# Two layers of linear attention and squared-ReLU MLP: a sixth row buffer, two row statistics traced into the last feature pair, and a norm's last transposes ordered behind the dense block's last rows

## The chip, the cores and the metric

The kernel runs on one core of one Trainium2 chip. The metric is the device time of one execution in microseconds (us). A profile of one execution gives, beside its time, every instruction of each engine: TensorE (PE), its weight loads (PEld), VectorE (DVE), ScalarE (ACT), GpSimd (POOL) and SyncE (SP), which issues most DMAs.

## The reference

The input has 2048 rows of 576 values. Two layers, with the same weights, follow one another; each is an attention part and a dense part, each behind a layer norm without gain, and added to its input.

```python
def _A_ref(x, wqkv, w_phi, wo):                 # H = 32 heads of Dh = 18
    q, k, v = ... x @ wqkv ...
    pq = einsum("bhsd,hdf->bhsf", q, w_phi); pk = einsum("bhsd,hdf->bhsf", k, w_phi)
    phi_q = concatenate([softmax(pq), softmax(-pq)]); phi_k = concatenate([softmax(pk), softmax(-pk)])
    kv = einsum("bhsf,bhsd->bhfd", phi_k, v); z = einsum("bhsf->bhf", phi_k)
    num = einsum("bhqf,bhfd->bhqd", phi_q, kv); den = einsum("bhqf,bhf->bhq", phi_q, z)[..., None] + 1e-6
    return (num / den) ... @ wo

def _B_ref(x, w1, b1, w2, b2):                  # F = 4608
    r = max(x @ w1 + b1, 0)
    return (r * r) @ w2 + b2

x = x + _A_ref(_layernorm(x), ...); x = x + _B_ref(_layernorm(x), ...)      # layer one
x = x + _A_ref(_layernorm(x), ...); x = x + _B_ref(_layernorm(x), ...)      # layer two
```

The attention has no causal mask: the sums kv and z of a layer need the keys and values of all 2048 rows before the first output row can be made.

## The kernel before, in words

**Tiling.** The 2048 rows are four blocks of 512, each of four row tiles of 128. A row tile is a buffer x of 128 partitions by 576 float32. For a matmul, every operand is split into a high part (rounded to the matmul's type) and a low part (the rest), and each product is made of three: high by high, high by low, low by high. The 4608 hidden values of the dense part are 36 features of 128.

**Order within a layer.** In layer one the blocks go in the order 3, 2, 0, 1 and in layer two in the order 1, 0, 3, 2. First comes the attention output of the order's first block (`barrier`). Then the dense part of that block (`g_mlp`) is traced, and into it the attention of the second block is woven (`back_first`), norm included. Then comes the dense part of the second block, with the attention of the third and fourth block woven in (`back_second`). Last come the dense parts of the third and fourth block together (`g_pair`). Its 18 steps (`products`, one for each pair of features) make the hidden values of both blocks with fewer products than two separate blocks would need, finish the third block's rows and put the fourth block's hidden values aside in memory; `seconds` then reads them back and makes the fourth block's down-projection, feature by feature, with loads of weights (m_pr, `load_wide`) and of hidden values (m_pg, `load_high`) three features ahead. In layer one, `back_keys` is woven into `seconds`: for the blocks 3, 2 and 0, which are finished by then, it makes layer two's norm, values v and keys k. In layer two nothing is woven there.

**What sets the order on an engine.** The order in which the program is traced gives priorities; a planner then lays out each engine's instructions by the time at which it reckons them ready. On top of that, `tc.issue_after(ins)` puts what is traced in its block behind `ins` on the engine of `ins`, without a wait between engines. `weave(main, other, rate)` traces one step of `main` after the other, each of which pays `rate`, and draws steps of `other`, each of which costs what it yields; what is left of `other` is traced at the end (`drain`). `chained` wraps a woven generator so that its instructions on DVE, ACT and POOL stay in the order in which they are traced, step behind step; its `strict` form, which `back_keys` has, also puts them behind the PE instruction that was traced last.

**Buffers.** Tiles of one tag take turns in a fixed number of buffers; a tile whose turn it is waits until the last user of the buffer's old tile is done. The row tiles have the tag "x", with five buffers: the rows of a norm, the rows to which the dense part's result is added (named x or m_px), and a few temporary tiles. In PSUM the tag "w" has two banks.

**The norm.** `g_norm` (L452) handles four row tiles. For each, `begin` fetches the row and takes two half statistics (L438) and their aggregate (L441) on DVE, and two small POOL steps. `scale` writes the normed row: four chunks of 128 columns (L469, named n_3n for block 3 of layer two) and the rest (L470, n_3e). `transpose` turns the four chunks on PE (L480, into n_3p) and `split_main` splits them into high (ACT, L488) and low (DVE, L489, n_3l); `transpose_rest` (L494) turns the rests of two row tiles. With `fine`, as in `back_keys`, these are separate steps: two statistics ahead of the first scaling, and always one ahead; each statistics step costs 2.0, each scaling 1.6, and behind them follow six crossings (0.3) and splits (0.9). Without `fine`, as for the norm at the end of an attention (`g_out`, L999), one step holds the scaling of one row tile and the transposes of the one before; the last of the five steps holds the fourth row tile's four transposes and the second two rests.

**The places that the change touches.** In `g_mlp` (L1189 to L1215) the last feature's rows are made by row tile: L1159 holds the matmuls of the row tiles (m_3acc for block 3), L1154 and L1150 those of the columns beyond 512 (`features`). Then come four transposes (L1209) and the additions to the rows (L1212 and L1214). L1132 makes the next dense block's hidden values (m_2ph). In `g_pair`, L1471 and L1481 are `features` and `by_rows`; in `last_rows`, m_px is loaded, gets its additions (L1516 and L1520) and is written to xs (L1522). The rows x0 to x3 of layer two's first norm (L1767) are those of block 3, written to xs long before; they share the buffers of tag "x" with the four m_px. In the main loop (L1848 to L1854) a first step of `back_keys` is drawn in the last of the 18 steps, behind the last low split of the hidden values (`paired`, L1463), and a second one behind the additions of L1516 (`added`):

```python
        for k, _ in enumerate(products):
            if k == NP - 1:
                with tc.issue_after(dense["paired"].ins):
                    next(back, None)
        with tc.issue_after(dense["added"].ins):
            next(back, None)
        weave(seconds, back, 0.85)
```

The weights of v (w_3v0h to w_3v1l, four pieces, L406) are drawn within `back_keys`, beside the norm's steps, by `g_load`, which puts each piece behind the DMA that was traced last on SP.

Of the kernel before, what the change touches and what calls it, by code (L numbers as in the profile page):

```python
# [21 lines left out]
def layers_kernel(  # L22
# [75 lines left out]
        for _ in gen:  # L98
            pass

    def weave(main, other, rate):

        due = 0.0
        for _ in main:
            due += rate
            while due >= 1.0:
                cost = next(other, other)
                if cost is other:
                    break
                due -= cost or 1.0  # L110
        drain(other)

    def pipeline(n, stages, costs):

# [674 lines left out]

    def phi_products(layer, e, name, tag="qk"):  # L790
        zb = sums[layer]["zb"]
        ms = [sb.tile([P, D], F32, tag=tag, name=f"{name}{s}", bufs=5) for s in range(2)]
        for s in range(2):
            (nc.gpsimd if s else nc.vector).tensor_mul(ms[s], e[:, s], zb[:, s])
        return ms
# [30 lines left out]
    def phi_late(layer, er, ph, name):  # L826

        zb, ms, us = sums[layer]["zb"], {}, {}
        for t in range(NT // 2, NT):
            ms[t] = [sb.tile([P, D], F32, tag="x", name=f"{name}m{t}{s}", bufs=5) for s in range(2)]  # L830
            us[t] = sb.tile([P, 2, H], F32, tag="u", name=f"{name}u{t}")
            ph.append(er[t][0])

        def product(t, s):
            return (nc.gpsimd if s else nc.vector).tensor_mul(ms[t][s], er[t][0][:, s], zb[:, s])

        def total(t, s):
            nc.vector.tensor_reduce(us[t][:, s], ms[t][s].rearrange("p (h d) -> p h d", d=DH), op=ALU.add, axis=AX.X)

        def factors(t):  # L840
            phi_factors(us[t], er[t][1])

        def scale(t, s):
            phi_scale(*er[t], (s,))

        return product, total, factors, scale
# [18 lines left out]
    def g_out(layer, b, ph, dst, name, parts=1, pause=None, behind=None, norm=None, mid=None, costs=(None, None)):  # L865
# [59 lines left out]
                return two + [wpiece(wo, HP, f"{name}o1", heads=True, low=nc.gpsimd)]  # L925

        def rows_in(t):
            x = sb.tile([P, D], F32, tag="x", name=f"{name}x{t}", bufs=5)
            nc.sync.dma_start(x, x_in[b * TB + t * P : b * TB + (t + 1) * P] if layer == 0 else xs[b][t])
            return x  # L930

# [64 lines left out]
            nc.sync.dma_start(xm[b][t], x)  # L996

        if not xs_of:
            yield from paced((norm or g_norm)(x_after, dst, f"{name}n", keep), costs[1])  # L999
            return  # L1000

        spare["tags"] = [f"acc{i}" for i in range(NC)]
# [87 lines left out]
    def g_mlp(layer, b, x, after, name, rest=None, then=None):  # L1090
# [108 lines left out]
        if then:  # L1199
            then()  # L1200
        for t in range(NT):
            x = sb.tile([P, D], F32, tag="x", name=f"{name}x{t}", bufs=5)
            nc.sync.dma_start(x, xm[b][t])
            after.append(x)
        by_rows(NF - 1, range(2), range(3))
# [1 line left out]
        p3 = pt.rearrange("p (t d) -> p t d", d=P)  # L1207
        for t in range(NT):
            nc.tensor.transpose(p3[:, t], yt[:, t * P : (t + 1) * P], ident)  # L1209
        by_rows(NF - 1, range(2, NT), range(3))  # L1210
        for t, x in enumerate(after):
            nc.vector.tensor_add(x[:, :R], acc[t][:, :R], x[:, :R])  # L1212
        for t, x in enumerate(after):
# [71 lines left out]
    def g_norm_second(x_of, dst, name, then):  # L1285

        ops, full, made = {}, [], {}

        def two(t):
            return t[:, : HK * TB].rearrange("p (c n) -> p c n", c=HK)  # L1290

        def prepare():
            rests = cst.tile([P, 2 * D], F32, name=f"{name}f", tag="zb")
            for a, k in enumerate(("b11", "b21")):
                cols = slice(a * HK * TB, (a + 1) * HK * TB)
                hi, lo = (sb.tile([P, 2 * D], F32, tag="E", name=f"{name}{k}{p}", bufs=4)[:, : HK * TB] for p in "hl")
                nc.sync.dma_start(hi, pth[:, cols])
                nc.sync.dma_start(lo, ptl[:, cols])
                full.append(rests[:TP, a * TB : (a + 1) * TB])
                nc.sync.dma_start(full[a], ptt[:, a * TB : (a + 1) * TB])  # L1300
                ops[k] = [two(hi.bitcast(F32R)), two(lo.bitcast(F32R))]

        def rest():
            for k in ("t1", "t3", "t4"):
                tags = ("wraw", "wraw") if k == "t4" else TAGS_A
                pair = [sb.tile([P, NC * HP], F32R, tag=tag, name=f"{name}{k}{p}", bufs=2)
                        for tag, p in zip(tags, "hl")]
                ops[k] = [two(p) for p in pair]
            x = xt_tiles(name)
            ops["b22"] = [x[p][:, :HK] for p in "hl"]  # L1310
            ops["t2"] = [x[p][:, HK:KC] for p in "hl"]
            for k in ("b11", "b21", "t1", "t2"):
                ops[k].append(sb.tile([GW, TB], F32R, tag="ft", name=f"{name}{k}t", bufs=4)[:TP])
            ops["t3"].append(sb.tile([P, TB], F32R, tag="olt", name=f"{name}t3t", bufs=1)[:TP])
            ops["t4"].append(sb.tile([P, KC * P], F32, tag="xn", name=f"{name}t4t").bitcast(F32R)[:TP])
            ops["b22"].append(x["h"][:TP, KC])
            for k, f in zip(("b11", "b21"), full):
                split_tail(ops[k][2], f)

        def split_tail(op, src):  # L1320
            nc.scalar.activation(op, src, AF.Copy)
            nc.vector.tensor_sub(op[TW : 2 * TW], src[TW : 2 * TW], op[TW : 2 * TW].bitcast(F32))

        def combine(new, c11, c21):
            b12, b22 = new
            temps = [sb.tile([P, D], F32, tag="x", name=f"{name}u{i}", bufs=5) for i in range(2)]
# [36 lines left out]

        prepare()
        yield from g_norm_halves(x_of, name, then, (main, split_main), (tail, split_tails), (0.3, 3.6, 2.4))
        dst.update(ops)

    def g_pair(layer, blocks, x, after, name):
# [120 lines left out]
        def last_rows(b):  # L1489
# [16 lines left out]
                nc.tensor.transpose(p3[:, t], yt[:, t * P : (t + 1) * P], ident)  # L1506
            xs_ = after if b else []
            for t in range(NT):
                xr = sb.tile([P, D], F32, tag="x", name=f"{name}x{b}{t}", bufs=5)
# [114 lines left out]

    def load_x(b):
        def get(t):
            x = sb.tile([P, D], F32, tag="x", name=f"x0_{b}_{t}", bufs=5)
# [118 lines left out]
    for layer in range(2):  # L1746
# [16 lines left out]

        def rows_of(b):
            def get(t):
                x = sb.tile([P, D], F32, tag="x", name=f"x1_{b}_{t}", bufs=5)
                nc.sync.dma_start(x, xs[b][t])  # L1767
                return x
            return get
# [66 lines left out]
                if last:  # L1836
                    keep.update(x=xk, es=es, v=wpair("v", f"w{m}"))

        weave(g_mlp(layer, order[0], ready, [], f"m{layer}_{order[0]}", dense.pop("rest")), chained(back_first()), 3.7)
        back = chained(back_second())  # L1840

        def then():
# [5 lines left out]
        for k, _ in enumerate(products):  # L1848
            if k == NP - 1:
                with tc.issue_after(dense["paired"].ins):  # L1850
                    next(back, None)
        with tc.issue_after(dense["added"].ins):
            next(back, None)
        weave(seconds, back, 0.85)  # L1854
# [35 lines left out]
```

## Time and profile before

| what | value |
|---|---|
| time, median of 3 runs | 2485.06 us (2484.94 to 2486.81) |
| the profiled execution's own time | 2485.37 us |
| its span, first to last instruction | 2483.7 us, 41469 instructions |
| mean granted TensorE clock | 0.999 of full speed |
| busy share of the span | PE 99%, PEld 87%, DVE 62%, ACT 51%, POOL 39% |
| moved by DMA | 348.67 MB, mean 140 GB/s |

The span holds the busy times, so what is taken from a row of the profile is compared with 2483.7 and, for the whole execution, with 2485.37. A row such as `1148.12 1.12 PE L480 MATMUL ... x4 [2.67 <-DVE n_3n L469]` gives the start of a group of like instructions and the time that they took together, in us; the engine and line of the program; output and inputs; the number of instructions; and, in brackets, how long the engine had stood before and what released it.

### The profile page before, as it was taken

To read this page: it belongs to the slowest core of one execution; us is meant where nothing else is said; L and a number is where in the kernel's file an instruction comes from. 1 tells how busy PE (TensorE), PEld (TensorE's weight loads), DVE (VectorE), ACT (ScalarE), POOL (GpSimd) and SP (SyncE) were. 2 spreads that over 40 slices of the span, in tenths; PEclk is the share of its full clock that TensorE was granted. 3 is DMA by queue.
4 is the path that set the end of the run, shared out by engine and by line. 5 is a ranking of instruction groups with operands and counts; after the bars stand their busy time and mean duration, and the time that the engine had idled before them with its cause. 6 is when DMAs were issued, how large, how long until landed. Compare 5 with 4: busy or idle time off the path is not lost.

```text
span 2483.7 us, 41469 instructions
## 1 busy us (share of the span) xinstructions
PE 2463.2 (99%) x15108; PEld 2169.5 (87%) x15108; DVE 1533.9 (62%) x2507; ACT 1262.1 (51%) x2243; POOL 959.3 (39%) x1101
## 2 busy tenths in 40 slices
PE   8999999999999999999999999999999999999999
PEld 8999888889888888888899988888888888888888
DVE  7778939364866655545656787584557665454454
ACT  4344545443546666664333445554445466666543
POOL 4445303212334665642433442132122355565322
PEclk9999999999999999999999999999999999999999
DMA  9124533356434433338753144333573444333363
GB/s 332 60 71 158 160 103 96 104 161 219 133 122 135 148 98 111 108 102 288 251 196 140 54 168 118 100 100 117 158 244 96 124 136 139 115 103 113 108 201 127
DMA packets 248891, 348.67 MB, mean 140 GB/s; under 512 B 30126, under 2 KB 155950, under 8 KB 246126
## 3 DMA queue, kind: packets, MB, share of 16 engines
q1 hardware_dynamic: 247428, 344.66, 44.1%
q8 instruction: 118, 1.93, 0.3%
q10 hardware_dynamic: 1258, 1.37, 0.2%
q14 instruction: 87, 0.71, 0.1%
HBM read 280.93 MB, written 65.00 MB: 139 GB/s over the span
## 4 chain that ended last, share of the span: by engine, by line
PE 94%; DVE 3%; DMA 1%; ACT 1%; issue 1%; POOL 0%; SPq 0%; ACTq 0%; DVEq 0%; POOLq 0%
PE m_ppx L1449 9%; PE m_pacc L1481 7%; PE m_pacacc L1481 5%; PE m_ppy L1449 5%; PE m_1ph L1132 5%; PE m_3ph L1132 5%; PE m_0ph L1132 5%; PE m_2ph L1132 5%; PE m_2acc L1159 4%; PE m_0acc L1159 4%; PE m_1acc L1159 3%; PE m_3acc L1159 3%; PE m_ppz L1449 2%; PE m_pacc L1471 2%; PE m_pacacc L1471 2%; PE m_pach L1481 2%
## 5 line engine op out<-in xcount | busy, mean ns | idle before, releaser
L1439 POOL TENSOR_TENSOR m_ps<-m_pr,m_ps 128x128 fp32r<-128x128 f32 x144 | 120.4, 836 | 329.7 <-ACT m_ps L1437 268.9
L1438 DVE TENSOR_TENSOR m_ps<-m_pr,m_ps 128x448 fp32r<-128x448 f32 x144 | 98.1, 681 | 187.4 <-ACT m_ps L1437 184.0
L1481 PE MATMUL m_pacc<-m_ps,m_phb 128*128 128x448 f32 x864 | 188.5, 366 | 0.0
L1481 PEld LDWEIGHTS m_pacc<-m_ps,m_phb 128*128 128x128 f32 x864 | 162.2, 188 | 18.1
L1437 ACT ACTIVATE m_ps<-m_pr 128x576 fp32r<-128x576 f32 x144 | 98.4, 683 | 133.0 <-issue 75.2
L1481 PE MATMUL m_pacacc<-m_ps,m_phc 128*128 128x448 f32 x648 | 150.1, 370 | 0.0
L1481 PEld LDWEIGHTS m_pacacc<-m_ps,m_phc 128*128 128x128 f32 x648 | 119.9, 189 | 9.2
L1159 PE MATMUL m_2acc<-m_2s,m_2hb 128*128 128x448 f32 x432 | 100.2, 366 | 0.0
L1159 PE MATMUL m_0acc<-m_0s,m_0hb 128*128 128x448 f32 x432 | 100.2, 366 | 0.0
L1159 PE MATMUL m_1acc<-m_1s,m_1hb 128*128 128x448 f32 x432 | 99.7, 365 | 0.0
L1159 PE MATMUL m_3acc<-m_3s,m_3hb 128*128 128x448 f32 x432 | 99.7, 365 | 0.0
L1132 PE MATMUL m_3ph<-t0onh,m_3h 128*128 128x512 f32 (+1 forms) x380 | 97.8, 383 | 0.5 <-ACT t0onh L488 0.5
L1132 PE MATMUL m_1ph<-t1onh,m_1h 128*128 128x512 f32 (+1 forms) x380 | 97.7, 382 | 0.5 <-ACT t1onh L488 0.5
L1132 PE MATMUL m_0ph<-a_0nh,m_0h 128*128 128x512 f32 (+1 forms) x380 | 97.7, 384 | 0.0
L1132 PE MATMUL m_2ph<-a_2nh,m_2h 128*128 128x512 f32 (+1 forms) x380 | 97.6, 384 | 0.0
L1159 PEld LDWEIGHTS m_0acc<-m_0s,m_0hb 128*128 128x128 f32 x432 | 80.9, 188 | 10.6 <-ACT m_0hb L1140 0.2
L1159 PEld LDWEIGHTS m_2acc<-m_2s,m_2hb 128*128 128x128 f32 x432 | 80.9, 188 | 10.5 <-ACT m_2hb L1140 0.2
L1159 PEld LDWEIGHTS m_1acc<-m_1s,m_1hb 128*128 128x128 f32 x432 | 81.1, 188 | 10.3
L1159 PEld LDWEIGHTS m_3acc<-m_3s,m_3hb 128*128 128x128 f32 x432 | 81.1, 188 | 10.3
L1117 POOL TENSOR_TENSOR m_3s<-m_3r,m_3s 128x128 fp32r<-128x128 f32 x36 | 24.2, 672 | 162.4 <-ACT m_3s L1111 148.2
L1117 POOL TENSOR_TENSOR m_1s<-m_1r,m_1s 128x128 fp32r<-128x128 f32 x36 | 24.1, 671 | 162.4 <-ACT m_1s L1111 148.1
L1132 PEld LDWEIGHTS m_3ph<-t0onh,m_3h 128*128 128x128 f32 x380 | 68.8, 188 | 14.0 <-ACT t0onh L488 0.7
(2440 smaller groups left out, 7296.3 us busy)
## 6 DMA issues: line engine op xcount, KB each, us to landing
m_pr<-in_B_w SPq DMA_DIRECT2D x144, 288.0 KB
m_pr<-in_B_w SPq DMA_DIRECT2D x72, 256.0 KB
hd<-m_pu SPq DMA_DIRECT2D x72, 256.0 KB
m_pg<-hd SPq DMA_DIRECT2D x72, 256.0 KB
m_3r<-in_B_w SPq DMA_DIRECT2D x36, 288.0 KB
m_2r<-in_B_w SPq DMA_DIRECT2D x36, 288.0 KB
m_1r<-in_B_w SPq DMA_DIRECT2D x36, 288.0 KB
m_0r<-in_B_w SPq DMA_DIRECT2D x36, 288.0 KB
```

The costliest lines, as they stand in the source:

```text
L1117: nc.gpsimd.tensor_sub(s2[:, D + R : 2 * D], r2[:, R:], s2[:, R:D].bitcast(F32))
L1132: dense["hidden"] = nc.tensor.matmul(ph[:, cols], a, m, start=(k == 0), stop=(k == len(ops) - 1))
L1159: nc.tensor.matmul(acc[t][:, :R], a[:, rows], m, start=(f == 0 and k == 0), stop=(f == NF - 1 and k == 2))
L1437: nc.scalar.activation(s2[:, :D], r2, AF.Copy)
L1438: nc.vector.tensor_sub(s2[:, D : D + R], r2[:, :R], s2[:, :R].bitcast(F32))
L1439: nc.gpsimd.tensor_sub(s2[:, D + R : 2 * D], r2[:, R:], s2[:, R:D].bitcast(F32))
L1449: nc.tensor.matmul(ps, a, m, start=start and i == 0, stop=i == len(ms) - 1, skip_group_check=True)
L1471: nc.tensor.matmul(accs[b][KC], a, m, start=(g == 0 and k == 0), stop=(g == NF - 1 and k == 2))
L1481: nc.tensor.matmul(accs[b][t][:, :R], a[:, rows], m, start=(g == 0 and k == 0), stop=(g == NF - 1 and k == 2))
```

## The change

Three things change.

1. Tag "x" has six buffers in place of five, at every place that uses it.
2. In the last step of the pair, two steps of `back_keys` are drawn in place of one. These are the statistics of the first two row tiles, x0 and x1. The step that is drawn behind `added` is then the scaling of x0, where it was the statistics of x1. In layer two nothing is drawn there, before or after.
3. In `g_out` without a norm of its own, that is in the attention of the order's second block in each layer, the fourth and fifth step of the norm yield 99.0 in place of 3.0. The weave cannot pay that, so the fifth step is left to its `drain`. For this weave the drain now stands under `issue_after(dense["rows"])`, the last PE instruction of the dense block's third row tile (number 2) in its last feature; row tiles 2 and 3, which were traced in one call, are traced in two.

```diff
-    def weave(main, other, rate):
+    def weave(main, other, rate, behind=None):
...
-        drain(other)
+        with tc.issue_after(dense[behind]) if behind else nullcontext():
+            drain(other)
...
         def rows_in(t):
-            x = sb.tile([P, D], F32, tag="x", name=f"{name}x{t}", bufs=5)
+            x = sb.tile([P, D], F32, tag="x", name=f"{name}x{t}", bufs=6)
...
         if not xs_of:
-            yield from paced((norm or g_norm)(x_after, dst, f"{name}n", keep), costs[1])
+            for i, cost in enumerate(paced((norm or g_norm)(x_after, dst, f"{name}n", keep), costs[1])):
+                yield cost if norm or i < NT - 1 else 99.0
             return
...
-        by_rows(NF - 1, range(2, NT), range(3))
+        by_rows(NF - 1, [2], range(3))
+        dense["rows"] = traced_on(nc.tensor)
+        by_rows(NF - 1, [3], range(3))
...
-        weave(g_mlp(layer, order[0], ready, [], f"m{layer}_{order[0]}", dense.pop("rest")), chained(back_first()), 3.7)
+        weave(g_mlp(layer, order[0], ready, [], f"m{layer}_{order[0]}", dense.pop("rest")), chained(back_first()), 3.7, "rows")
...
             if k == NP - 1:
                 with tc.issue_after(dense["paired"].ins):
-                    next(back, None)
+                    for _ in range(2):
+                        next(back, None)
```

The other lines of the diff change `bufs=5` to `bufs=6` for the same tag, in the temporary tiles of the attention's products, in the rows of `g_mlp` and `g_pair`, in `load_x` and in `rows_of` (L1767).

More of the change, by code (lines that the diff above doesn't have):

```diff
@@ L791, in phi_products @@
         zb = sums[layer]["zb"]
-        ms = [sb.tile([P, D], F32, tag=tag, name=f"{name}{s}", bufs=5) for s in range(2)]
+        ms = [sb.tile([P, D], F32, tag=tag, name=f"{name}{s}", bufs=6 if tag == "x" else 5) for s in range(2)]
         for s in range(2):
@@ L829, in phi_late @@
         for t in range(NT // 2, NT):
-            ms[t] = [sb.tile([P, D], F32, tag="x", name=f"{name}m{t}{s}", bufs=5) for s in range(2)]
+            ms[t] = [sb.tile([P, D], F32, tag="x", name=f"{name}m{t}{s}", bufs=6) for s in range(2)]
             us[t] = sb.tile([P, 2, H], F32, tag="u", name=f"{name}u{t}")
@@ L1201, in g_mlp @@
         for t in range(NT):
-            x = sb.tile([P, D], F32, tag="x", name=f"{name}x{t}", bufs=5)
+            x = sb.tile([P, D], F32, tag="x", name=f"{name}x{t}", bufs=6)
             nc.sync.dma_start(x, xm[b][t])
@@ L1325, in combine @@
             b12, b22 = new
-            temps = [sb.tile([P, D], F32, tag="x", name=f"{name}u{i}", bufs=5) for i in range(2)]
+            temps = [sb.tile([P, D], F32, tag="x", name=f"{name}u{i}", bufs=6) for i in range(2)]
             t1, t2, t3, t4 = (t[: b12.shape[0], i * HK * P : (i + 1) * HK * P] for t in temps for i in range(2))
@@ L1508, in last_rows @@
             for t in range(NT):
-                xr = sb.tile([P, D], F32, tag="x", name=f"{name}x{b}{t}", bufs=5)
+                xr = sb.tile([P, D], F32, tag="x", name=f"{name}x{b}{t}", bufs=6)
                 nc.sync.dma_start(xr, xm[blocks[b]][t])
@@ L1626, in get @@
         def get(t):
-            x = sb.tile([P, D], F32, tag="x", name=f"x0_{b}_{t}", bufs=5)
+            x = sb.tile([P, D], F32, tag="x", name=f"x0_{b}_{t}", bufs=6)
             nc.sync.dma_start(x, x_in[b * TB + t * P : b * TB + (t + 1) * P])
@@ L1765, in get @@
             def get(t):
-                x = sb.tile([P, D], F32, tag="x", name=f"x1_{b}_{t}", bufs=5)
+                x = sb.tile([P, D], F32, tag="x", name=f"x1_{b}_{t}", bufs=6)
                 nc.sync.dma_start(x, xs[b][t])
```

## The prediction
> **What bounds the kernel now.** First the page's head and its busy table.
>
> ```profile
> span 2483.7 us, 41469 instructions
> PE 2463.2 (99%) x15108; PEld 2169.5 (87%) x15108; DVE 1533.9 (62%) x2507; ACT 1262.1 (51%) x2243; POOL 959.3 (39%) x1101
> ```
>
> TensorE (PE) is the bound in every stretch: 2483.7 less 2463.2 leaves 20.5 us of idle time in all. A change that keeps every matmul, as this one does, can only win idle time of PE, or time at a low clock. So the next view is PE's own waits, longest first.
>
> ```profile
> PE n_3p L480 <- DVE n_3n L469: 2.7, 1, 2.7
> PE a_2np L480 <- DVE a_2nn L469: 0.6, 1, 0.6
> PE a_0np L480 <- DVE a_0nn L469: 0.6, 1, 0.6
> ...
> PE n_2p L494 <- DVE n_2l L489: 0.4, 1, 0.4
> ```
>
> The first three are the waits that the diff can reach. The first is the first transposes of layer two's first norm (rows x0 to x3 of block 3, loaded in L1767), while the pair's second half (seconds) runs. The other two are the fourth row tile's transposes in the norm of the order's second block, one in each layer. The fourth is the next norm of layer two, woven in the same way. Next PE in order of time around the first wait, and the granted clock there.
>
> ```profile
> 1144.69 0.77 PE L1481 MATMUL m_pach<-m_ps,m_phc 128*128 128x448 f32 x3
> 1148.12 1.12 PE L480 MATMUL n_3p<-ident,n_3n 128*128 128x128 f32 x4 [2.67 <-DVE n_3n L469]
> 1148.89 2.21 PE L1481 MATMUL m_pacacc<-m_ps,m_phc 128*128 128x448 f32 x5
> 1150.90 0.75 PE L480 MATMUL n_3p<-ident,n_3n 128*128 128x128 f32 x4
> 1151.41 1.06 PE L1481 MATMUL m_pacacc<-m_ps,m_phc 128*128 128x448 f32 x4
> ...
> 1153.61 1.40 PE L1481 MATMUL m_pacacc<-m_ps,m_phc 128*128 128x448 f32 x6
> 1154.84 0.38 PE L494 MATMUL n_3p<-ident,n_3e 128*128 128x128 f32 x2
> ...
> 1156.13 1.04 PE L480 MATMUL n_3p<-ident,n_3n 128*128 128x128 f32 x8
> 1156.93 0.47 PE L1471 MATMUL m_pacacc<-m_phc,m_ps 128*128 128x512 f32 x1
> ...
> 1159.05 0.84 PE L571 MATMUL v_3pv<-w_3v0h,n_3h 128*128 128x288 f32 x5
> ```
>
> ```profile
> 1148.00:1150.00 2.00, 1.88 (x7) 1.79 (x8) 1.97 (x8) 0.60 (x1) 1.25 (x4) 0.50 0.96 270
> ...
> 1152.00:1155.00 3.00, 3.00 (x18) 2.61 (x16) 2.49 (x7) 1.53 (x3) 1.61 (x4) 1.00 1.05 401
> ```
>
> The two rows of the last view give busy time and instructions of PE, its weight loads, DVE, ACT and POOL, then the granted clock, the DMA engines' busy share and GB/s. PE stands for 2.67 us and then runs at a clock of 0.50. From start to start, at full clock a transpose takes 0.10 us (1156.13 to 1156.93, eight) and a row matmul 0.205 (1153.61 to 1154.84, six). Behind the wait, four transposes take 0.77 instead of 0.40, five row matmuls 2.01 instead of 1.03, four transposes 0.51 instead of 0.40: 1.46 us lost to the clock. This site costs 2.67 + 1.46 = 4.13 us.
>
> Why n_3n is late is seen on VectorE (DVE), on SyncE (SPq) and in the chain of waits.
>
> ```profile
> 1131.29 0.81 DVE L438 BATCH_NORM_STATS2 n_3s<-x 128x6 f32<-128x288 f32 x2
> ...
> 1133.68 2.42 DVE L1516 TENSOR_TENSOR m_px<-m_pacc,m_px 128x448 f32<-128x448 f32 x4
> 1136.02 0.87 DVE L1520 TENSOR_TENSOR m_px<-m_ppy,m_px 128x128 f32<-128x128 f32 x4
> ...
> 1146.59 0.82 DVE L438 BATCH_NORM_STATS2 n_3s<-x 128x6 f32<-128x288 f32 x2 [2.32 <-DMA x<-xs]
> 1147.45 0.21 DVE L441 BATCH_NORM_AGGREGATE n_3m<-n_3s 128x2 f32<-128x12 f32 x1
> 1147.57 0.49 DVE L469 TENSOR_SCALAR n_3n<-x,n_3m,n_3d 128x512 f32<-128x512 f32 x1
> 1147.98 0.34 DVE L470 TENSOR_SCALAR n_3e<-x,n_3m,n_3d 128x128 f32<-128x128 f32 x1
> ```
>
> ```profile
> 1124.97 0.42 SPq L406 DMA_DIRECT2D w_3v0h<-wsvh  x1
> ...
> 1134.48 0.43 SPq L406 DMA_DIRECT2D w_3v1l<-wsvl  x1
> 1136.33 2.88 SPq L1522 DMA_DIRECT2D xs<-m_px  x4
> 1143.72 1.71 SPq L1767 DMA_DIRECT2D x<-xs  x3
> 1145.54 0.37 SPq L1435 DMA_DIRECT2D m_pr<-in_B_w  x1
> ```
>
> ```profile
> 1137.47 7.62 DMA xs<-m_px
> 1145.54 4.91 DMA m_pr<-in_B_w
> ```
>
> x0's statistics are ready at 1132, but in the chained order of the norm x1's statistics stand ahead of x0's scaling. The five x buffers are full (x0 and the four m_px), so x1 is loaded only when the first m_px has been written out: at 1143.72, with its data used at 1146.59, 2.87 us later. Only then comes L469 on x0, long known.
>
> **The change, part by part.** *Two statistics and the sixth buffer.* x1 now has a buffer beside x0 and the m_px, is loaded early and gets its statistics behind x0's. The step behind "added" becomes x0's scaling: 0.49 + 0.34 us of DVE right after 1136.9. x0's buffer is then free, and x2 takes it: x2's load no longer waits for a write of m_px. Issued near 1138.8 among those writes, it lands 2.87 us later (as x1 above) to 7.62 (as the write), 1141.7 to 1146.4; I take the short end. x3 is the first load that waits for a write.
>
> The draw moves too: each step of seconds pays 0.85, statistics cost 2.0, scaling 1.6, a crossing 0.3. With x0's scaling drawn outside, the first crossing is drawn at the 12th step of seconds in place of the 14th, in the third feature, before PE's row of 1144.69, and its input has been there for 5 us. I count the 4.13 us as won.
>
> Its price: x1's two half statistics and their aggregate (0.82 + 0.21, from the rows at 1146.59) move ahead of L1516 on DVE, and their two small POOL steps ahead of low parts of weights. The adds at 1133.68 come 1.0 us later, which delays PE's new accumulators.
>
> ```profile
> 1135.89 1.99 PE L1481 MATMUL m_pacacc<-m_ps,m_phc 128*128 128x448 f32 x9
> ```
>
> These nine matmuls need the bank that the first add frees: at 1133.68 + 2.42/4 = 1134.3 before, 1135.3 after, 0.6 us in time; the next two follow at the same pace. With that cover gone it would cost 0.4. I count 0.
>
> SP: the x3 load is drawn at the 6th step, the weight pieces of v (w_3v0h to w_3v1l) from the 10th, and each piece is put behind the last traced DMA. That was a hidden-state load of seconds (so 1124.97), and is now x3's load, which must wait for m_px to be written. So four pieces move from 1124.97..1134.48 to behind about 1140. That empties the queue ahead of the writes (7.62 us then) and fills it behind them.
>
> ```profile
> w_3v0h<-wsvh SPq DMA_DIRECT2D x1, 720.0 KB
> ```
>
> The writes start 1.0 us late, at 1137.3. x3's load can start between 1140.2 (2.87 us, the x row) and 1144.9 (7.62). I take the short end again, since the pieces (size below) are gone from ahead of them. v_3pv uses the pieces at 1159.05, or at 1154.9 with the 4.13 won: 10 us and more behind. I count 0 here and keep the loss as a rival.
>
> *The last transposes.* In layer 0:
>
> ```profile
> 507.22 1.18 PE L1159 MATMUL m_3acc<-m_3s,m_3hb 128*128 128x448 f32 x5
> 508.97 0.66 PE L480 MATMUL a_2np<-ident,a_2nn 128*128 128x128 f32 x4 [0.57 <-DVE a_2nn L469]
> ...
> 510.25 1.46 PE L1159 MATMUL m_3acc<-m_3s,m_3hb 128*128 128x448 f32 x6
> 511.54 0.75 PE L1132 MATMUL m_2ph<-a_2nh,m_2h 128*128 128x256 f32 x5
> ```
>
> ```profile
> 508.25 0.67 DVE L469 TENSOR_SCALAR a_2nn<-a_2x,a_2nm,a_2nd 128x512 f32<-128x512 f32 x1 [0.43 <-POOL a_2nd L443]
> ...
> 511.07 0.68 DVE L489 TENSOR_TENSOR a_2nl<-a_2np,a_2nh 128x512 fp32r<-128x512 f32 x1
> ```
>
> The six transposes go behind row tile 2. At 508.4 (507.22 + 1.18) PE then has a row matmul, the four transposes of L1209 and three to six row matmuls: at 0.2 us for a row and 0.1 for a transpose 1.2 us or more, while the wait is 0.57. So 0.57 is won per layer, 1.14 in all. What comes late next: a_2nl at 511.07, now behind the four L1212 adds. The next block's second feature needs the PSUM bank that it frees. The first feature's early half covers it: 14 matmuls of 256 columns, five of which take 0.75 at 511.54, the last one's tail included, so some 1.7 us. Ends 0 and 0.5 per layer; I take 0.1, nearer to 0 because of that cover.
>
> *The sixth buffer elsewhere* lets x loads leave earlier. No row of PE's waits names an x load in those stretches, so I count 0, with ends of 0.6 each way, the largest wait left in the middle of the kernel.
>
> *Sum.* 4.13 + 1.14 - 0.20 = 5.07 us. The profiled execution took 2485.37 (1.67 around the span), 0.31 above the median of 2485.06. So 2480.3 by the profile, 2480.0 by the median.
>
> *The clock, weighed.* By the rows, an idle time of 2.67 us brought 0.50 at 1148. The Trainium skill (TensorE: Matmul & The Clock Gate, Part 1, "What's actually happening") says that the clock halves after an idle window of about 3.4 us. The trace does not agree: 2.67 was enough. By that rule the 1.46 us would not belong to the wait, and the sum would be 3.6.
>
> **The rivals.**
>
> *The wait moves on.* x3 still waits for a write, and the splits stand behind x3's scaling in DVE's order. Free PSUM banks, and so the third crossing, wait for them. The order was laid out too early by 2.67 us for such a write and load. For it: that write is still in the path. Against: the queue ahead is emptier. All of the wait stays: only 0.94 is won, 2484.1; half of it without the low clock: 2481.3.
>
> *Slower: the weight pieces crowd out the dense rows' loads.* 4 x 720 KB at the 401 GB/s of a full queue (the window from 1152) are 7.4 us of all DMA engines, now just as m_pr and m_pg are loaded (the load of 1145.54 already took 4.91). It decides when PE reaches the feature or v_3pv before its weights have landed. PE then idles up to 7.4 in place of 2.67, and pays two windows of half clock instead of one: +4.73 + 1.46 - 0.94, so 2490.3. For it: the DMA share of 0.96 in the window quoted. Against: weights lie three features ahead.
>
> *It doesn't do what it says.* The planner finds the transposes ready in its model and leaves the order nearly as it is: 2485.
>
> *The low clock stays* though the wait goes (the skill's rule, by which 2.67 us cannot have caused it): 2481.5. The rows speak against it.
>
> **How the numbers follow.** About 0.2%, 5.0 us, is what a measurement of this kernel can tell from no change; the forecast lies on that bound. Forecast 0.44 (0.31 beyond the bound, 0.13 short of it), the wait moves 0.25, slower 0.20, nothing 0.06, clock 0.03, a further gain from earlier loads 0.02. Faster 0.31 + 0.02 = 0.33; same 0.13 + 0.25 + 0.06 + 0.03 = 0.47; slower 0.20. The range goes from 2478.8 (the forecast, less the 0.2 taken off, the side gain of 0.6 and the n_2p wait of 0.4) to 2486.0, which takes in all but the slower rival. Cases of both signs hold much of the chance: the forecast's own range is 2478.8 to 2481.5.
>
> **What would show it.** Right: PE's wait on n_3n gone, the clock full from 1140 to 1160, x1's statistics near 1132.4, L469 on x0 near 1138, w_3v0h issued after 1140; no wait on a_2nn and a_0nn, and the transposes of row tile 3 behind row tile 2 of the dense block. Wrong: a wait of n_3p (L480 or L494) or v_3pv over 1 us anywhere from 1140 to 1165, a clock of 0.50 there, dense rows waiting for m_ps, or a wait of m_2ph and m_0ph for a PSUM bank.

## The result and the profile after

The changed kernel takes 2481.07 us (median of 16 runs, 2478.94 to 2483.54), the kernel before 2486.75 us (16 runs beside them, 2484.94 to 2489.19). The ratio is 0.9979, with a 95% interval of 0.9972 to 0.9986. The forecast, 2480.0 from a median of 2485.06, was a ratio of 0.9980. The profiled execution of the changed kernel took 2478.94 us, the shortest of the 16. Its page begins:

```profile
span 2477.2 us, 41454 instructions
...
PE 2460.7 (99%) x15108; PEld 2168.0 (88%) x15108; DVE 1538.2 (62%) x2507; ACT 1261.8 (51%) x2243; POOL 962.0 (39%) x1101
```

PE's waits, longest first, whole execution. Lines of the program have moved by one to four: L469 is L470, L489 is L490, L1481 is L1485, L1767 is L1771.

```profile
PE fp L283 <- DMA fr<-in_A_wqkv: 2.6, 2, 1.7
...
PE n_3p L495 <- DVE n_3l L490: 0.6, 1, 0.6
```

The waits on n_3n, a_2nn, a_0nn and n_2l are gone. What is left at the first site is 0.6 us, at the third crossing. PE in order of time there, and then the busy times and the clock, which is 1.00 all the way from 1140 to 1160:

```profile
1141.58 0.60 PE L481 MATMUL n_3p<-ident,n_3n 128*128 128x128 f32 x4
...
1144.19 0.66 PE L481 MATMUL n_3p<-ident,n_3n 128*128 128x128 f32 x4
...
1148.55 0.41 PE L495 MATMUL n_3p<-ident,n_3e 128*128 128x128 f32 x2 [0.60 <-DVE n_3l L490]
...
1152.74 0.82 PE L572 MATMUL v_3pv<-w_3v0h,n_3h 128*128 128x288 f32 x5
```

```profile
1145.00:1150.00 5.00, 4.40 (x25) 3.72 (x24) 4.46 (x11) 1.55 (x3) 1.43 (x3) 1.00 0.97 383
```

DVE and SyncE show why. x1's statistics are taken at 1131, x0 is scaled right behind the additions, and the two low splits (L490), on which the third crossing waits for a PSUM bank, stand behind x3's scaling, as the prediction's first rival described. But x3's scaling did not wait for a write, as that rival has it: DVE stood 0.51 us for a POOL step of the norm there.

```profile
1131.02 0.77 DVE L439 BATCH_NORM_STATS2 n_3s<-x 128x6 f32<-128x288 f32 x2
...
1135.82 0.54 DVE L470 TENSOR_SCALAR n_3n<-x,n_3m,n_3d 128x512 f32<-128x512 f32 x1
...
1147.01 0.55 DVE L470 TENSOR_SCALAR n_3n<-x,n_3m,n_3d 128x512 f32<-128x512 f32 x1 [0.51 <-POOL n_3d L444]
...
1147.72 1.28 DVE L490 TENSOR_TENSOR n_3l<-n_3p,n_3h 128x512 fp32r<-128x512 f32 x2
```

```profile
1123.75 0.42 SPq L407 DMA_DIRECT2D w_3v0l<-wsvl  x1
...
1127.92 0.39 SPq L379 DMA_DIRECT2D t1q0r<-wf  x1
...
1135.34 3.14 SPq L1526 DMA_DIRECT2D xs<-m_px  x4
1138.58 1.13 SPq L1771 DMA_DIRECT2D x<-xs  x2
1139.76 0.48 SPq L407 DMA_DIRECT2D w_3v0h<-wsvh  x1
1140.29 0.42 SPq L407 DMA_DIRECT2D w_3v1h<-wsvh  x1
1140.75 0.43 SPq L407 DMA_DIRECT2D w_3v1l<-wsvl  x1
```

Three of v's four pieces have moved behind x3's load; w_3v0l has not. Loads of layer two's query weights (t1q0r, t1q1r), which stood far behind in the kernel before, have moved ahead of the writes of m_px. The writes are quick: by the trace the first lands 3.98 us after its issue, against 7.34 before. x2's load, issued at 1138.58 without waiting for a write, lands 3.53 us later.

The execution falls into stages whose ends are fixed PE instructions. All times are from the two profiles, in us.

| stage | before | after | won |
|---|---|---|---|
| start to the first dense matmul (m_3ph) | 233.65 | 232.74 | 0.91 |
| to the first pair's product, one moved set of transposes within | 581.25 | 581.00 | 0.25 |
| to the first m_pach | 320.38 | 320.30 | 0.08 |
| fourth block's down-projection, from there to a fixed matmul in its 36th feature (at 1340.07 before, 1333.98 after) | 204.79 | 199.94 | 4.85 |
| layer two from its first transposes (t1onp) to PE's last matmul, the other moved set within | 1021.21 | 1020.86 | 0.35 |

These add up to 6.44; the two spans differ by 6.43. The stretch between the last two rows (118.47 and 118.48) and what follows PE's last matmul (3.90 in both) are left out. The first row is chance: that stage, which the change leaves alone, took 232.7 to 236.6 us over 14 profiled executions of all the kernels here. The third row is of the same kind (320.3 to 320.9).

### The profile page after: what moved, and what is told of

The parts are those of the page before. It is cut to its first block, busy times and chain, and to the rows that moved or that the text cites. A ratio compares the mean times of both kernels' runs of the same rounds, so it can differ in the third digit from the quotient of the medians.

```text
span 2477.2 us, 41454 instructions
## 1 busy us (share of the span) xinstructions
PE 2460.7 (99%) x15108; PEld 2168.0 (88%) x15108; DVE 1538.2 (62%) x2507; ACT 1261.8 (51%) x2243; POOL 962.0 (39%) x1101
## 4 chain that ended last, share of the span: by engine, by line
PE 95%; DVE 3%; ACT 1%; issue 0%; DMA 0%; POOL 0%; SPq 0%; ACTq 0%; DVEq 0%; POOLq 0%
PE m_ppx L1453 9%; PE m_pacc L1485 7%; PE m_pacacc L1485 5%; PE m_ppy L1453 5%; PE m_1ph L1134 5%; PE m_3ph L1134 5%; PE m_0ph L1134 5%; PE m_2ph L1134 5%; PE m_2acc L1161 4%; PE m_0acc L1161 4%; PE m_3acc L1161 4%; PE m_1acc L1161 4%; PE m_ppz L1453 2%; PE m_pacc L1475 2%; PE m_pacacc L1475 2%; PE m_pach L1485 2%
## 5 line engine op out<-in xcount | busy, mean ns | idle before, releaser
L1485 PE MATMUL m_pacc<-m_ps,m_phb 128*128 128x448 f32 x864 | 188.5, 366 | 0.0
L1485 PEld LDWEIGHTS m_pacc<-m_ps,m_phb 128*128 128x128 f32 x864 | 162.1, 188 | 18.1
L1485 PE MATMUL m_pacacc<-m_ps,m_phc 128*128 128x448 f32 x648 | 149.1, 368 | 0.0
L1485 PEld LDWEIGHTS m_pacacc<-m_ps,m_phc 128*128 128x128 f32 x648 | 119.2, 188 | 9.2
L1161 PEld LDWEIGHTS m_1acc<-m_1s,m_1hb 128*128 128x128 f32 x432 | 81.1, 188 | 10.3
L1119 POOL TENSOR_TENSOR m_2s<-m_2r,m_2s 128x128 fp32r<-128x128 f32 x36 | 28.1, 781 | 136.5 <-ACT m_2s L1113 128.8
```

Of the source, the lines that this page charges most:

```text
L1119: nc.gpsimd.tensor_sub(s2[:, D + R : 2 * D], r2[:, R:], s2[:, R:D].bitcast(F32))
L1161: nc.tensor.matmul(acc[t][:, :R], a[:, rows], m, start=(f == 0 and k == 0), stop=(f == NF - 1 and k == 2))
L1485: nc.tensor.matmul(accs[b][t][:, :R], a[:, rows], m, start=(g == 0 and k == 0), stop=(g == NF - 1 and k == 2))
```

## The experiments

In what follows "the stage" is the fourth row of that table. It is the sharper instrument: three executions with the change's buffer and statistics, and nothing else done to that norm, took 199.94, 199.94 and 199.93, while a whole execution varies by 4 to 6 us and a ratio of runs is known to 0.0009. Where a ratio is given it is to the kernel before, run on the same chip, with its 95% interval.

**The parts of the change.** The moved transposes alone:

```diff
-        drain(other)
+        with tc.issue_after(dense[behind]) if behind else nullcontext():
+            drain(other)
...
+                yield cost if norm or i < NT - 1 else 99.0
```

> The kernel before with the last transposes of the second block's norm put behind the dense block's row tile 2, and nothing else of the change. Theory A (the gains of the change add up, each from its own wait): PE's waits on a_2nn and a_0nn, 0.57 us each, are gone, PE's wait of 2.67 us on n_3n and the clock of 0.50 behind it stay, and the time falls by 0.6 to 1.0 us, ratio 0.9996 to 0.9998. Rival B (the moved transposes shift what is drawn later, so that this part carries part of the gain in the fourth block's down-projection): the n_3n wait changes too and the gain is over 1.5 us.

Ratio 1.0002 (0.9993 to 1.0011), an interval that holds theory A's 0.9996 to 0.9998 as well as no change. The moved transposes did as theory A has it: 580.98 and 1020.87 in the second and last stage, 0.27 and 0.34 less than before. But the n_3n wait was gone too, against theory A, in a stage whose instructions stand in the same order as before. PE's waits in it:

```profile
PE k_3kp L572 <- DMA w_3k1l<-wskl: 1.6, 1, 1.6
PE n_3p L495 <- DVE n_3l L490: 1.1, 2, 0.9
```

The chain of waits has the third write of m_px, 7.62 us in the kernel before's profile, at 4.83:

```profile
1138.72 4.83 DMA xs<-m_px
```

So the wait of 2.67 us was one draw. With quick writes it vanished, and 1.6 us came back at w_3k1l; the stage took 203.01.

The buffer with two statistics, and the buffer alone:

```diff
-            x = sb.tile([P, D], F32, tag="x", name=f"{name}x{t}", bufs=5)
+            x = sb.tile([P, D], F32, tag="x", name=f"{name}x{t}", bufs=6)
...
-                    next(back, None)
+                    for _ in range(2):
+                        next(back, None)
```

> The kernel before with the sixth buffer and the two statistics in the last pair, without the moved transposes. Theory A: the wait on n_3n and the low clock behind it are gone, a wait of about 0.6 us at the third crossing stays as in the changed kernel, the waits on a_2nn and a_0nn of 0.57 us stay; the time falls by 4.0 to 5.5 us, ratio 0.9979 to 0.9984. Rival B: under 3.5 us, the rest being due to the transposes.

Ratio 0.9985 (0.9976 to 0.9994), a little less than theory A's 0.9979 to 0.9984 but with those within the interval; stage 199.94. The wait of 0.6 us at the third crossing and those on a_2nn and a_0nn of 0.6 us stayed. Theory A holds.

> The kernel before with the sixth buffer alone. Theory A1 (x1's late load alone made x0's scaling late; with a sixth buffer x1 is loaded ahead of the writes of m_px, so its statistics wait for nothing even where one step is drawn in the last pair): the wait on n_3n is gone, the clock stays full, and the time falls by 3 to 5 us, ratio 0.9980 to 0.9988. Theory A2, as the prediction put it (the buffer only serves the second statistics; what counts is that x0's scaling is drawn behind the additions): a wait on n_3n of over 1 us stays and less than 2 us is won.

Ratio 0.9999 (0.9990 to 1.0008), stage 203.34. The wait moved from the first crossing to the second, where x1's scaling stands behind x2's statistics; x2's load landed 5.72 us after its issue, behind writes of 6.1 to 6.6:

```profile
PE n_3p L480 <- DVE n_3n L469: 1.6, 1, 1.6
PE n_2p L480 <- issue: 1.0, 1, 1.0
PE k_3kp L571 <- DMA w_3k1l<-wskl: 0.4, 1, 0.4
```

These are A2's numbers, but not its reason: x1's early load did remove x1's wait, and x2's took its place.

> The changed kernel once more, beside its parts on the same chip. By its runs so far: ratio 0.9972 to 0.9986, 3.5 to 7 us less than before. If the parts add up (theory A), its gain is that of the moved transposes alone plus that of the buffer with the two statistics, within 0.5 us.

Ratio 0.9981 (0.9972 to 0.9989), stage 199.93. The parts add up: against the buffer with two statistics it is shorter by 0.31 in the second stage and 0.37 in the last.

**The kernel before once more.**

> The kernel before once more, for its profile. Theory I (the wait of 2.67 us and the low clock behind it hang on how long the writes of m_px take in the execution that is profiled, 7.3 to 7.6 us there and 4.6 to 5.0 in the run with the moved transposes alone, whose program is the same there): with short writes the wait on n_3n is under 0.5 us and a wait of 1 to 2 us stands on w_3k1l instead; the down-projection takes 202.5 to 205 us. Rival J (the wait is fixed): 2.5 to 2.9 us on n_3n and 204.6 to 205.

One run, 2488.91; the stage took 207.88, longer than either theory allowed, with 3.41 us of half clock behind the wait on w_3k1l. PE's waits in it:

```profile
PE n_3p L494 <- DVE n_3l L489: 2.0, 2, 1.8
PE k_3kp L571 <- DMA w_3k1l<-wskl: 1.9, 1, 1.9
PE n_3p L480 <- DVE n_3n L469: 1.2, 1, 1.2
```

With the writes at 5.9 to 6.3 us the n_3n wait was 1.2, and the other two grew. So one order of instructions in this stage gave 203.0, 204.8 and 207.9. Theory I is right that the wait hangs on the writes, not that the stage stays within 205.

**The place of v's pieces.** The changed kernel with the pieces back ahead of the writes:

```diff
-            with tc.issue_after(traced_on(nc.sync)):
+            with tc.issue_after(at or traced_on(nc.sync)):
...
+                if t == 2 and b == order[0]:
+                    dense["sync"] = traced_on(nc.sync)
```

> The changed kernel, with the four pieces of v's weights put back ahead of the writes of m_px on SyncE's queue, where the kernel before has them. Theory E (the change gains also by an emptier queue ahead of the writes, as the prediction counted): the writes take 6 to 7.6 us in place of 4.0 to 4.9, x2's data come 1.5 to 3 us later, the wait on n_3l at the third crossing grows from 0.6 to 2 us or more, and the down-projection takes 201.5 us or more. Rival F (other loads stand where the pieces were, the 512-partition-row loads of t1q0r and t1q1r, so the queue is as full either way): the writes take 4 to 5 us and the down-projection 199.6 to 200.6.

Ratio 0.9989 (0.9980 to 0.9998), stage 203.68. The pieces came out some 5 us earlier than in the kernel before, the first 15.2 us ahead of the stage's start (1119.09) against 10.3 (1124.97), but ahead of the writes as meant. By the trace the writes took 6.8 to 7.5 us. SyncE's wait for them, which is that of x3's load, PE's waits in the stage, and DVE where the second crossing's input is made:

```profile
SPq L1773 <- DMA xs<-m_px: 3.3, 1, 3.3
```

```profile
PE n_3p L481 <- DVE n_3n L470: 2.4, 1, 2.4
PE k_3kp L572 <- DMA w_3k1l<-wskl: 1.2, 1, 1.2
```

```profile
1145.23 0.82 DVE L439 BATCH_NORM_STATS2 n_3s<-x 128x6 f32<-128x288 f32 x2 [2.26 <-DMA x<-xs]
1146.09 0.21 DVE L442 BATCH_NORM_AGGREGATE n_3m<-n_3s 128x2 f32<-128x12 f32 x1
1146.21 0.49 DVE L470 TENSOR_SCALAR n_3n<-x,n_3m,n_3d 128x512 f32<-128x512 f32 x1
```

Theory E holds, though the wait stood at the second crossing and not the third. x1's scaling stands behind x2's statistics, and x2's load, which waits for no write, stands behind the writes on the queue: issued at 1138.37, it landed 6.85 us later, 0.72 behind the last write. 3.74 of the 4.85 us are lost again, with the buffer and the two statistics still in place; the waits of 2.4 and 1.2 are nearly all of it. This is one profile. The ten runs point the same way, but their interval (0.9980 to 0.9998) overlaps with the change's. And the other way round, the kernel before with nothing but the pieces behind x3's load:

```diff
-            with tc.issue_after(traced_on(nc.sync)):
+            with tc.issue_after(at or traced_on(nc.sync)):
...
                 nc.sync.dma_start(x, xs[b][t])
+                if t == NT - 1 and b == order[0]:
+                    dense["sync"] = traced_on(nc.sync)
```

> The kernel before, with five buffers, one step in the last pair and the old order of the norm, but with the four pieces of v's weights put behind x3's load on SyncE's queue. In the order that results, the loads of t1q0r and t1q1r take their place ahead of the writes, and w_3k1h and w_3k1l come ahead of the x rows of block 0, as in the changed kernel. Theory K (the place of the pieces carries most of the gain; the buffer and the second statistics bring it about by moving x3's load ahead of them in the trace): the writes of m_px take 4 to 5 us, the wait on n_3n is at most 0.5 us, none stands on w_3k1l, a wait of about 1 us is left at the third crossing, and the down-projection takes 200.5 to 201.7 us, against 203.0 to 207.9 in three executions of the old order and 199.94 in the changed kernel. Theory L (the early load of x1 and the scaling of x0 carry it): 203 us or more.

Ratio 0.9987 (0.9978 to 0.9996), stage 200.78: theory K, but for a wait of 0.8 on n_3n where at most 0.5 was expected, and one of 0.4 at the third crossing where about 1 was. The first row is from the chain of waits, the others are PE's waits in the stage; w_3k1l is not among them.

```profile
1137.24 4.65 DMA xs<-m_px
```

```profile
PE n_3p L480 <- DVE n_3n L469: 0.8, 1, 0.8
PE n_3p L494 <- DVE n_3l L489: 0.4, 1, 0.4
PE n_2p L494 <- DVE n_2l L489: 0.4, 1, 0.4
```

With the sixth buffer in addition, one step in the last pair as before:

> The kernel before with the sixth buffer and with v's four pieces behind x3's load, one step in the last pair. Theory K1 (once the pieces are out of the way, the buffer gives the rest, 0.8 us, by x1's early load, and the second statistics in the last pair nothing): no wait on n_3n at the first crossing, the down-projection takes 199.7 to 200.2 us. Theory K2 (the second statistics are needed for the rest): a wait of 0.5 us or more on n_3n, 200.5 to 201 us, as with the pieces moved alone (200.78).

One run, 2482.98; stage 201.24, a little above K2's 200.5 to 201, so the buffer alone gave nothing; K2 is right that the second statistics are needed. x2's load waited for a write (4.70 us in the chain of waits), and x1's scaling behind it:

```profile
PE n_3p L480 <- DVE n_3n L469: 1.2, 1, 1.2
```

Stage times by the two factors:

| | v's pieces ahead of the writes | behind x3's load |
|---|---|---|
| five buffers, one step | 204.79, 207.88, 203.01 | 200.78 |
| six buffers, one step | 203.34 | 201.24 |
| six buffers, two steps | 203.68 | 199.94, 199.94, 199.93 |

In the last cell w_3v0l is ahead, as the change has it; the 203.01 is of the kernel with the moved transposes, which lie outside the stage. The pieces do not move alone: where they stand behind, the loads of t1q0r and t1q1r stand ahead of the writes, and w_3k1l's load ahead of block 0's rows. The wait on w_3k1l is there in every profile of the left column and in none of the right one. The wait on n_2l is there in every profile of the first two rows and in none of the last, so that it goes with the second statistics.

**Another order of the norm.** Five buffers, x0's scaling ahead of x1's statistics, without and with the pieces moved:

```diff
-            if t + 1 < NT:
+            if t + 1 < NT and fine != "lone":
                 start(t + 1)
...
+            if t + 1 < NT and fine == "lone":
+                start(t + 1)
+                yield 2.0
```

> The kernel before, with five buffers and one step in the last pair, but in layer two's first norm x0 is scaled ahead of x1's statistics, so that the step behind the additions is x0's scaling. Theory C (x0's scaling is late only because x1's statistics, and so x1's load behind a write of m_px, stand ahead of it in the chained order; the buffer itself is not needed for that): no wait on n_3n at the first crossing, whatever the writes take; x1 to x3 still come behind the writes, so a wait of 0.5 to 2 us moves to a later crossing. The fourth block's down-projection (first m_pach to the 36th feature), 204.79 us in the kernel before's profile and 199.94 in the changed kernel's, takes 201 to 203. Rival D (the second early load is what counts): a wait of over 1.5 us on n_3n of x1 or later, and 203.5 or more.

> The same with x0 scaled ahead of x1's statistics in addition, still with five buffers. Theory K: with quick writes and x0's scaling drawn behind the additions, nothing of the first crossing waits; the down-projection takes 200 to 201 us, and the sixth buffer, which alone left 203.34, is worth less than 1 us once the pieces are out of the way. Theory L (x1's load ahead of the writes is needed): waits of over 1.5 us on n_3n and n_3l as without the pieces moved, 202.5 us or more.

Ratios 0.9999 (0.9990 to 1.0007) and 0.9998 (0.9990 to 1.0007), stages 203.85 and 204.28. The first kernel had no wait at the first crossing, as theory C says, but 1.8 us each at the second and third, in theory D's range; the second refutes what theory K gave for it and lies in theory L's range. The kernel with the pieces moved shows a cost that none of the theories had: with no statistics one ahead, every scaling stands for POOL's two small steps. DVE there:

```profile
1148.84 0.55 DVE L469 TENSOR_SCALAR n_3n<-x,n_3m,n_3d 128x512 f32<-128x512 f32 x1 [0.99 <-POOL n_3d L443]
...
1152.08 0.55 DVE L469 TENSOR_SCALAR n_3n<-x,n_3m,n_3d 128x512 f32<-128x512 f32 x1 [1.00 <-POOL n_3d L443]
...
1154.85 0.67 DVE L469 TENSOR_SCALAR n_3n<-x,n_3m,n_3d 128x512 f32<-128x512 f32 x1 [1.00 <-POOL n_3d L443]
```

In part theory L's reason is there too: by the trace x1's load landed 5.15 us after its issue, and DVE stood 1.05 us for it. So these two kernels cannot say what the early scaling alone is worth.

**What is left at the third crossing.** The changed kernel with two crossings and splits ahead of x3's scaling:

```diff
+            elif fine == "split":
+                for step, cost in ((cross, 0.3), (split, 0.9)):
+                    for i in range(2):
+                        step(i)
+                        yield cost
             apart(t)
...
```

> The changed kernel with the first two crossings and splits of layer two's first norm traced ahead of x3's scaling. Theory G (the 0.6 us wait that is left stands for PSUM banks that the splits free, and the splits are held up only by x3's load and scaling ahead of them in the chained order): the wait on n_3l at the third crossing, 0.6 us and 0.2 around it, is gone, and the down-projection takes 199.0 to 199.4 us instead of 199.94. Rival H (x3's scaling is then late in its turn): the wait comes back at the fourth or fifth crossing, 199.8 or more.

Stage 199.25, 0.69 less than the change; the transposes of the rests start without a wait, at 1148.41:

```profile
1148.41 0.41 PE L495 MATMUL n_3p<-ident,n_3e 128*128 128x128 f32 x2
```

Theory G holds. Ratio 0.9979 (0.9970 to 0.9988), against 0.9981 for the change: the runs cannot tell the two apart. The same splits with five buffers, the pieces moved and the transposes moved:

> The kernel before with five buffers and one step in the last pair, with v's four pieces behind x3's load, the first two crossings and splits ahead of x3's scaling, and the moved transposes. Theory K: the wait at the third crossing goes as in the kernel with the early splits (0.69 us there), the wait of about 0.8 us on n_3n at the first crossing stays or grows by the splits' share of DVE; the down-projection takes 200.0 to 200.9 us, and the time is within 1.5 us of the changed kernel's: ratio 0.9979 to 0.9988. Rival M (the early splits push x3's scaling behind more of DVE's work where x1 comes late): 201.5 us or more.

Ratio 0.9982 (0.9973 to 0.9991), stage 200.11, a wait of 0.7 on n_3n: theory K. Within what runs can tell, this has the change's gain without its buffer and its second statistics.

## Why the prediction was right, and where it was not

**The size.** 5.07 us were forecast, 5.68 measured by the medians. That they are so near is in part luck: the first site's price was one draw, and the terms that the sum did not have went both ways. Of the 6.43 between the profiles the forecast's two terms, the first site and the moved transposes, cover the stages that won 4.85, 0.25 and 0.35; the 0.99 in the other two are chance.

**The first site: right size, the cause on the wrong step.** x0 was scaled behind the additions, the first crossing came in the third feature and its input was there, as forecast. But the prediction put the 4.13 us to the buffer and the statistics and counted the moved pieces at 0. By the table, the pieces' place gave 3.7 us with the change's norm and 2.2 to 7.1 with the old one. Buffer and second statistics together gave 0.84 on top of it; without it, 203.68 against 203.01 to 207.88, anything from a loss of 0.7 to a gain of 4.2, by the draw of the kernel before. Most cells hold a single profile, and the runs say the same more weakly: the pieces moved alone gave 0.9987, clear of 1, and the change with the pieces early 0.9989 against its own 0.9979 and 0.9981. The step that failed is "I count 0 here". The prediction had seen that the queue is emptied ahead of the writes, and gave that as its reason for the short end of x3's load. For x2's load, on which the second crossing hangs, it took the short end without that reason: 3.53 us with the pieces moved, 6.85 with them ahead. With the pieces ahead, the wait moved on, as rival one says: 2.4 us at the second crossing.

**Terms that it did not have.** A wait of 0.60 at the third crossing (1.03 against the usual spacing of PE's matmuls, from 1143.69 to 1148.55) was counted at 0 in the sum; the first rival named its place and the splits as its cause. On the other side the waits on w_3k1l and n_2l went, 0.60 and 0.89 by the same measure:

```profile
PE n_2p L494 <- DVE n_2l L489: 0.4, 1, 0.4
PE k_3kp L571 <- DMA w_3k1l<-wskl: 0.3, 1, 0.3
```

w_3k1l's load now stands ahead of block 0's rows in SyncE's order, as it does in the kernel with the pieces moved alone, which has no wait on it either. That gain outweighs the new wait: 4.13 less 1.03, and 0.60 and 0.89 added, are 4.59 of the 4.85 that the stage won. Where the other 0.26 came from is not shown.

**One execution's price.** 2.67 + 1.46 was the price in the execution that was shown. In two others the same place cost 1.2 with full clock, or nothing, with 1.8 or 0.9 at the third crossing and 1.6 to 1.9 at w_3k1l. In the three executions with the change's norm the stage took the same within 0.01, with a first write of 3.98 to 4.50 us, so the gain is larger where the draw of the kernel before is worse. That is no proof against a slow draw: with slow writes (the pieces early) the same norm lost most of it. The runs of before spread over 2482.8 to 2489.7, those of the change over 2478.9 to 2483.5.

**The transposes.** From a_2np's third set to the next block's first transposes (a_0pt) the time fell from 12.34 (505.85 to 518.19) to 11.87 (504.98 to 516.85): 0.47, the forecast's net term. The rows of before, then those of after:

```profile
505.85 0.60 PE L480 MATMUL a_2np<-ident,a_2nn 128*128 128x128 f32 x4
...
518.19 0.27 PE L895 MATMUL a_0pt<-ident,a_0Q0e 128*126 128x128 f32 x1
```

```profile
504.98 0.60 PE L481 MATMUL a_2np<-ident,a_2nn 128*128 128x128 f32 x4
...
509.80 0.84 PE L1134 MATMUL m_2ph<-a_2nh,m_2h 128*128 128x256 f32 x5
...
516.85 0.27 PE L896 MATMUL a_0pt<-ident,a_0Q0e 128*126 128x128 f32 x1
```

That the net term was met is luck, since neither part was. Up to the first m_2ph (511.54 before) 0.87 was won where 0.57 was forecast, and m_2ph's matmuls then took 7.05 in place of 6.65, 0.40 where 0.1 was taken, within the ends of 0 and 0.5. Over the whole stage 0.25 and 0.35 were left; where the rest went is not shown. The sum was 0.94 and is 0.60.

**No loss.** The price on DVE did not arise: the additions were to come 1.0 us later, but they start 1.69 us ahead of the first m_pach (1132.35), against 1.60 before, and the first write is issued 1.30 behind it, against 1.05. The pieces did not crowd out the dense rows. m_pr's load behind them took 9.4 us by the trace and no row waited for it; the last piece landed 2.8 us ahead of v_3pv at 1152.74. That rival's condition, a wait on a weight, never arose in the changed kernel.

## What to carry to other kernels

A load that is put behind "whatever was traced last on this queue" has an accidental place; when an edit moves a draw, look up where such loads go, because here the place of three or four loads of 720 KB, ahead of four writes of 288 KB or behind them, was worth more than the buffer. Price a wait that ends on a DMA from several executions, not from one. And before changing an order, see what the old one hides: one set of statistics ahead hid up to 1.0 us of POOL at a scaling.

## What the runs showed of the hardware

The clock did not go by the length of a wait. In the kernel before 2.67 us were followed by a clock of 0.50; in the changed kernel with the pieces early 2.45 us were not:

```profile
1144.00:1147.00 3.00, 0.55 (x4) 0.24 (x3) 1.73 (x6) 0.63 (x1) 0.53 (x2) 1.00 0.98 312
1147.00:1150.00 3.00, 3.00 (x18) 2.81 (x17) 2.49 (x7) 1.17 (x2) 1.84 (x4) 1.00 0.98 367
```

A wait of 1.2 us in layer one's first attention was followed by a clock of 0.50 in the kernel with the moved transposes alone, and by full clock in the changed kernel. The rows are the former's and the latter's:

```profile
219.00:222.00 3.00, 3.00 (x15) 3.00 (x15) 2.17 (x8) 1.97 (x6) 1.40 (x1) 0.50 0.00 0
```

```profile
218.00:221.00 3.00, 2.92 (x24) 2.55 (x22) 2.54 (x9) 2.90 (x8) 1.73 (x2) 1.00 0.00 0
```

Every low stretch within the kernels, ahead of their last matmuls, lasted 3.41 us, whatever the wait. And by the traces' record of the granted clock, all changes of the clock in an execution lie on one grid. From the first rise of the clock, 6.8 to 13.6 us into the span, to every later change there is a whole number of steps of 3.41333 us, to within 0.001 of a step, in all 14 profiles: 334 steps to the drop at 1147.79 in the kernel before, 62 to the one at 218.72 in the kernel with the moved transposes alone, 347 to the one at 1193.20 in the second profile of the kernel before. The Trainium skill (TensorE: Matmul & The Clock Gate, Part 1, "What's actually happening") says that activity is judged in a free-running window of 3413 ns. The runs agree with that.

So a wait counts by where it falls on the grid. Of the 2.67 us, 2.33 fell into one step, and the clock dropped at that step's end. The 2.45 us fell into two, with 0.92 and 1.52 us of idle time in them, and it did not. Idle time alone does not decide it, though: in the first attention, steps with 1.40 to 1.45 us of it were followed by the half clock in six profiles and steps with 1.42 to 1.44 were not in three others, nor was one with 1.79 at the norm. What else counts is open. The Trainium skill's idle window of about 3.4 us, in the same section, was not needed: a wait of 1.2 us was enough in those six, beside shorter waits close by. The prediction's 1.46 us of low clock was therefore a draw as well.
